# Attention in blocks of 32 queries by 64 keys, and three engines in written order, ahead of a PReLU feed-forward

## The chip, the cores and the metric

The kernel runs on one core of one Trainium2 chip. The metric is the time of one execution on the device in microseconds (us). Before the change it is 992.74 us, the median of 3 runs (988.51 to 993.65). Five engines work side by side: PE (TensorE, matrix products; PEld are its weight loads), DVE (VectorE), ACT (ScalarE), POOL (GpSimd) and SP, which issues the DMAs.

## The reference

Eight batches of 576 tokens, 8 heads of 64. Heads 0 to 3 look back at the last 32 positions, heads 4 to 7 at every fourth of the last 128. A feed-forward of 512 x 2048 x 512 with a PReLU follows.

```python
scores = scale * np.matmul(q, k.transpose(0, 1, 3, 2))
mask_plain = (rel >= 0) & (rel < window)                                   # window = 32
mask_dil = (rel >= 0) & (rel < window * dilation) & (rel % dilation == 0)  # dilation = 4
scores = np.where(masks[None, :, :, :], scores, -1000000000.0)
attn = np.exp(scores - np.max(scores, axis=-1, keepdims=True))
attn = attn / (np.sum(attn, axis=-1, keepdims=True) + 1e-09)
attn_out = np.matmul(attn, v)
...
h = x @ w_in                                          # x: 4608 x 512
g = np.maximum(h, 0.0) + alpha * np.minimum(h, 0.0)
return g @ w_out
```

## The kernel before

**Feed-forward.** The 4608 tokens are cut into 9 tiles of 512, the 2048 hidden values into 16 chunks, so there are 144 steps; step n is tile n // 16, chunk n % 16. `ffn_h` (L259) makes one 128 x 512 block of h with 12 matmuls (4 chunks of the model width, 3 passes each: every fp32 operand is kept as a high and a low fp32r part, and high x high, high x low and low x high are added). `ffn_g` (L264 to L277) applies the PReLU and casts the high part of g on ACT, `ffn_low` (L283) subtracts the low part on DVE, and `ffn_y` (L291) adds g's chunk to four output blocks with 12 matmuls. y runs one step behind h while tile 0 is done, two steps behind after that. After chunk 15 four blocks go out by DMA.

**Attention.** The work is cut by batch, pair of heads c (4 of them; the two heads lie on the lower and upper 64 partitions) and half u of the sequence: 64 units of 3 blocks, each block 96 queries by 128 keys. For the dilated heads tokens are sorted by residue modulo 4 beforehand, so that both kinds are a band. A unit goes through `scores` (L124, 6 fp32 matmuls; the profile shows each as two MATMUL records), `maxima` (L139, DVE adds the mask and takes the maximum), `exponentials` (L148, ACT), `divisions` (L155 to L158, DVE), `transposes` (L165, 6 on PE), `copies` (L170, ACT), `values` (L177, 6 fp32 matmuls), `highs` (L210, ACT) and `lows` (L214, DVE), which write the high and low parts of x.

**Weights.** They arrive as float64 in 32 chunks of 512 KB, and `convert_weight` (L238 to L247) makes each into a high and a low fp32r chunk: a magnitude on ACT (L238), four operations on the two words on DVE (L239, L240, L242, L244), the high cast on ACT (L246), the low part on DVE (L247).

**Order.** Batch 0 runs ahead of the first step, with 4 of the 32 conversions beside it. The 16 steps of tile 0 carry the other 28, two a step, and the 8 units of batch 1. From step 16 on a step is 24 matmuls of the feed-forward, and two steps share one unit of attention until batch 7 is through. The order on PE, DVE and ACT is set by a scheduler from the order of the code, so independent instructions are mixed; each engine then runs its queue in order. PSUM has 8 banks: four under the tag "y" (the output blocks; before step 1 the scores of batch 0) and four under "a" (h, scores, transposes and values, in rotation: a new tile takes the bank of the fourth tile before it). Weights in their float64 form and g share four buffers (tag "g"). DMAs wait in the queue of SP.

Of the kernel before, what the change touches and what calls it, by code (L numbers as in the profile page):

```python
# [9 lines left out]
F32 = mybir.dt.float32  # L10
# [12 lines left out]
BQ = 96  # L23
NBLK = S // BQ
UB = 3
UQ = UB * BQ
# [17 lines left out]
F64_HIGH = float.fromhex("0x1.dffffep16")  # L44


@with_exitstack
def tile_window_attention_prelu_ffn(
# [29 lines left out]
    ident = const.tile([BQ, BQ], F32, name="ident")  # L78
    make_identity(nc, ident)
    mask_sb = const.tile([BQ, NMASK, P], F32, name="mask_sb")  # L80
    al = const.tile([P, NF], F32, name="al")
    nal = const.tile([P, NF], F32, name="nal")
    wi = const.tile([P, 2, NF, NC, P], F32R, name="wi")
# [11 lines left out]
    keys = {}  # L95

    class Unit:
        def __init__(self, b, c, u, banks="a", room=None):
            self.b, self.c, self.u, self.banks = b, c, u, banks
            self.plain = 2 * c < HP  # L100
            self.blocks = range(UB * u, UB * (u + 1))
            self.starts = PLAIN_START if self.plain else DIL_START
            self.kinds = PLAIN_KIND if self.plain else DIL_KIND
            self.id = f"{b}_{c}_{u}"
            self.room = room

        def load(self):
            b, c, u = self.b, self.c, self.u
            if u == 0:
                keys[b, c] = att.tile([P, S], F32, tag="k", name=f"k_{b}_{c}")  # L110
                nc.sync.dma_start(out=keys[b, c], in_=kT[b, c])
            self.k = keys[b, c]
            self.q = att.tile([P, UQ], F32, tag="q", name=f"q_{self.id}", bufs=3)
            nc.sync.dma_start(out=self.q, in_=qT[b, c, :, u * UQ:(u + 1) * UQ])
            self.v = att.tile([P, 2, UB, D], F32, tag="v", name=f"v_{self.id}", bufs=3)
            nc.sync.dma_start(out=self.v, in_=vW[b, c, u])

        def scores(self):

            self.ps = [psp.tile([BQ, UB, P], F32, tag=self.banks, name=f"s_{self.id}_{e}") for e in range(2)]  # L120
            for i, j in enumerate(self.blocks):
                for e in range(2):
                    rows = slice(e * D, (e + 1) * D)
                    nc.tensor.matmul(  # L124
                        self.ps[e][:, i, :], lhsT=self.q[rows, i * BQ:(i + 1) * BQ],
                        rhs=self.k[rows, self.starts[j]:self.starts[j] + P], start=True, stop=True,
                    )

        def maxima(self):

            self.nm = sml.tile([BQ, 2, UB], F32, tag="nm", name=f"nm_{self.id}")
            if self.room is not None:
                self.pr = self.room
            else:
                pr = [att.tile([BQ, UB, P], F32, tag="pr", name=f"pr_{self.id}_{e}", bufs=3) for e in range(2)]
                self.pr = pr
            for e in range(2):
                for i, j in enumerate(self.blocks):
                    nc.vector.tensor_tensor_reduce(  # L139
                        out=self.pr[e][:, i, :], in0=self.ps[e][:, i, :], in1=mask_sb[:, self.kinds[j], :],  # L140
                        scale=-SCALE, scalar=3.0e38, op0=ALU.add, op1=ALU.min, accum_out=self.nm[:, e, i:i + 1],
                    )

        def exponentials(self):
            self.sm = sml.tile([BQ, 2, UB], F32, tag="sm", name=f"sm_{self.id}")
            for e in range(2):
                for i in range(UB):
                    nc.scalar.activation(  # L148
                        out=self.pr[e][:, i, :], in_=self.pr[e][:, i, :], func=AF.Exp,
                        bias=self.nm[:, e, i:i + 1], scale=-1.0, accum_out=self.sm[:, e, i:i + 1],  # L150
                    )

        def divisions(self):
            rs = sml.tile([BQ, 2, UB], F32, tag="rs", name=f"rs_{self.id}")
            nc.vector.tensor_scalar_add(rs, self.sm, 1e-9)  # L155
            nc.vector.reciprocal(out=rs, in_=rs)
            for e in range(2):
                nc.vector.tensor_tensor(  # L158
                    out=self.pr[e], in0=self.pr[e], in1=rs[:, e, :, None].broadcast_to([BQ, UB, P]), op=ALU.mult)

        def transposes(self):
            self.tp = [psp.tile([P, UB, BQ], F32, tag="a", name=f"t_{self.id}_{e}") for e in range(2)]
            for e in range(2):
                for i in range(UB):
                    nc.tensor.transpose(out=self.tp[e][:, i, :], in_=self.pr[e][:, i, :], identity=ident)  # L165
# [294 lines left out]
```

## Time and profile before

| | before |
|---|---|
| median of 3 runs | 992.74 us (988.51 to 993.65) |
| the profiled execution | 995.82 us |
| its span, first to last instruction | 993.9 us |
| DVE busy / ACT busy in the span | 580.9 us / 382.9 us |
| mean granted TensorE clock | 0.972 |
| moved by DMA | 58.78 MB |

The profile is of one execution, on the one core. Busy time is the time in which an instruction of the engine runs, "PEclk" the share of full clock that TensorE was granted. In the lists of groups a row has the line, the engine, the operation, output <- inputs, the shape, the count, busy time and the mean of one. A timeline row has start, duration and what ran, with the idle time before it and what ended that in brackets.

### The profile page before, as it was taken

The page shows a single profiled execution, that of the slowest core. Times are in us where ns is not written, and L with a number is a line of the kernel's source. Part 1 is how long each engine was busy: PE and PEld are TensorE (multiplying, and loading weights), DVE is VectorE, ACT ScalarE, POOL GpSimd, SP SyncE. Part 2 cuts the span into 40 slices and gives each one's busy share as a digit, 9 for nine tenths or more (in the row PEclk, how much of TensorE's full clock was granted, in tenths as well). Part 3 has the DMA queues.
Part 4 walks back from the last instruction along what each step waited for, and adds up shares of the span by engine and source line. Part 5 has one row for each costly group of instructions (what it writes and reads, how often), then busy time and mean ns, then how long its engine had stood idle before and what let it go on. Part 6 is the DMA issues. An engine that isn't in the chain of part 4 may idle for free.

```text
span 993.9 us, 14724 instructions
## 1 busy us (share of the span) xinstructions
PE 964.2 (97%) x5388; PEld 770.4 (78%) x5388; DVE 580.9 (58%) x1732; ACT 382.9 (39%) x1267; POOL 0.6 (0%) x6
## 2 busy tenths in 40 slices
PE   7699999999999999999999999999999999999998
PEld 4466766788888888888888888888888888888886
DVE  5869899755555556655555556555555544434343
ACT  5757667533433334433343334333433321111111
POOL 0000000000000000000000000000000000000000
PEclk8579899999999999999999999999999999999999
DMA  7334543211112111211121112111121001001001
GB/s 234 116 104 163 164 156 125 83 41 40 41 38 67 33 41 40 83 41 41 41 82 36 32 41 83 41 41 40 41 74 32 1 1 43 1 1 43 0 1 43
DMA packets 39303, 58.78 MB, mean 59 GB/s; under 512 B 3808, under 2 KB 28480, under 8 KB 39232
## 3 DMA queue, kind: packets, MB, share of 16 engines
q1 hardware_dynamic: 39232, 57.84, 18.6%
q8 instruction: 43, 0.70, 0.3%
q14 instruction: 28, 0.23, 0.1%
HBM read 48.39 MB, written 9.44 MB: 58 GB/s over the span
## 4 chain that ended last, share of the span: by engine, by line
PE 88%; DVE 7%; ACT 2%; issue 1%; DMA 1%; SPq 0%; ACTq 0%
PE h L259 38%; PE y L291 37%; PE s L124 5%; PE o L177 4%; PE t L165 3%; DVE wa L244 1%; DVE wa L242 1%; DVE wa L239 1%; DMA q<-qT 1%; DVE pr L139 1%; ACT early L148 1%; DVE wi L247 1%; DVE pr L158 1%; DVE wo L247 1%; DVE m L271 1%
## 5 line engine op out<-in xcount | busy, mean ns | idle before, releaser
L291 PE MATMUL y<-g,wo 128*128 128x512 f32 x1728 | 431.1, 397 | 7.2 <-ACT g L277 7.2
L259 PE MATMUL h<-x,wi 128*128 128x512 f32 x1728 | 427.4, 397 | 0.0
L259 PEld LDWEIGHTS h<-x,wi 128*128 128x128 f32 x1728 | 331.2, 192 | 69.8 <-issue 0.4
L291 PEld LDWEIGHTS y<-g,wo 128*128 128x128 f32 x1728 | 315.8, 188 | 81.4 <-ACT g L277 10.6
L274 DVE TENSOR_SCALAR m<-h,al 128x512 f32<-128x512 f32 x128 | 96.1, 751 | 278.8 <-PE h L259 274.2
L277 ACT CAST g<-m 128x512 fp32r<-128x512 f32 x144 | 89.5, 621 | 188.5 <-DVE m L275 185.8
L283 DVE TENSOR_TENSOR g<-m,g 128x512 fp32r<-128x512 f32 x144 | 99.1, 688 | 55.8 <-ACT g L277 55.6
L148 ACT ACTIVATE pr<-pr,nm 96x128 f32<-96x128 f32 x336 | 130.8, 392 | 2.3 <-DVE nm L139 2.2
L210 ACT CAST x<-o 128x288 fp32r<-128x288 f32 (+8 forms) x112 | 36.0, 393 | 218.3 <-PE o L177 218.3
L170 ACT COPY pt<-t 128x288 f32<-128x288 f32 x128 | 46.2, 400 | 141.7 <-PE t L165 141.2
L275 DVE SCALAR_TENSOR_TENSOR m<-h,m 128x512 f32<-128x512 f32 x128 | 88.5, 692 | 4.4
L139 DVE CUSTOM_DVE_ANT_0 pr<-s,mask_sb 96x128 f32<-96x128 f32 x336 | 75.2, 281 | 0.0
L124 PE MATMUL s<-k,q 64*96 64x128 f32 x768 | 62.2, 290 | 5.1 <-DMA q<-qT 5.1
L148 ACT ACTIVATION_READ_ACCUMULATOR pr<-pr,nm 96x1 f32 x336 | 63.6, 189 | 0.0
L158 DVE TENSOR_TENSOR pr<-pr,rs 96x384 f32<-96x384 f32 x112 | 57.7, 550 | 1.7
L124 PEld LDWEIGHTS s<-k,q 64*96 64x96 f32 x768 | 47.1, 165 | 14.8 <-issue 6.7
L177 PEld LDWEIGHTS o<-pt,v 128*64 128x64 f32 x768 | 37.2, 143 | 23.9 <-issue 20.5
L177 PE MATMUL o<-pt,v 128*64 128x96 f32 x768 | 50.9, 264 | 0.6 <-ACT pt L170 0.2
L165 PEld LDWEIGHTS t<-ident,pr 96*128 96x128 f32 x336 | 34.4, 142 | 15.2 <-DVE pr L158 8.1
L165 PE MATMUL t<-ident,pr 96*128 96x96 f32 x336 | 40.2, 252 | 4.2 <-DVE pr L158 4.1
L214 DVE TENSOR_TENSOR x<-o,x 128x288 fp32r<-128x288 f32 (+8 forms) x112 | 41.4, 383 | 3.7 <-ACT x L210 3.7
L139 DVE DVE_READ_ACCUMULATOR2_ANT nm<- 96x1 f32 x384 | 30.4, 79 | 0.0
(33 smaller groups left out, 281.6 us busy)
## 6 DMA issues: line engine op xcount, KB each, us to landing
v<-vW SPq DMA_DIRECT2D x64, 192.0 KB, 2.3
k<-kT SPq DMA_DIRECT2D x32, 288.0 KB, 3.2
q<-qT SPq DMA_DIRECT2D x64, 144.0 KB, 2.8
out<-ob SPq DMA_DIRECT2D x36, 256.0 KB, 2.2
ws<-w_in SPq DMA_DIRECT2D x16, 512.0 KB, 3.6
ws<-w_out SPq DMA_DIRECT2D x16, 512.0 KB, 3.5
mask_sb<-masks SPq DMA_DIRECT2D x1, 144.0 KB, 3.6
al<-alpha SPq DMA_DIRECT2D x1, 8.0 KB, 3.2
```

The costliest lines, as they stand in the source:

```text
L124: nc.tensor.matmul(self.ps[e][:, i, :], lhsT=self.q[rows, i * BQ:(i + 1) * BQ], rhs=self.k[rows, self.starts[j]:self.starts[j] + P], start ...
L139: nc.vector.tensor_tensor_reduce(out=self.pr[e][:, i, :], in0=self.ps[e][:, i, :], in1=mask_sb[:, self.kinds[j], :], scale=-SCALE, scalar= ...
L148: nc.scalar.activation(out=self.pr[e][:, i, :], in_=self.pr[e][:, i, :], func=AF.Exp, bias=self.nm[:, e, i:i + 1], scale=-1.0, accum_out=s ...
L158: nc.vector.tensor_tensor(out=self.pr[e], in0=self.pr[e], in1=rs[:, e, :, None].broadcast_to([BQ, UB, P]), op=ALU.mult)
L165: nc.tensor.transpose(out=self.tp[e][:, i, :], in_=self.pr[e][:, i, :], identity=ident)
L177: nc.tensor.matmul(self.po[e * D:(e + 1) * D, i, :], lhsT=self.v[:, e, i, :], rhs=self.pt[e][:, i, :], start=True, stop=True,)
L259: nc.tensor.matmul(ps, lhsT=wi[:, a, f, c, :], rhs=x[:, c, e, :], start=(n == 0), stop=(n == 3 * NC - 1))
L274: nc.vector.tensor_scalar(out=m, in0=ps, scalar1=0.0, scalar2=al[:, f:f + 1], op0=ALU.min, op1=ALU.mult)
L275: nc.vector.scalar_tensor_tensor(out=m, in0=ps, scalar=0.0, in1=m, op0=ALU.max, op1=ALU.add)
L277: nc.scalar.copy(out=g[:, 0, :], in_=m)
L283: nc.vector.tensor_tensor(out=g[:, 1, :], in0=ms.pop((t, f)), in1=g[:, 0, :].bitcast(F32), op=ALU.subtract)
L291: nc.tensor.matmul(ys[t][c], lhsT=wo[:, a, f, c * P:(c + 1) * P], rhs=g[:, e, :], start=(f == 0 and n == 0), stop=(f == NF - 1 and n == 2),)
```

## The change

1. Attention is cut into blocks of 32 queries by 64 keys, and a pair of heads of one batch (`Pair`, both halves at once) takes the place of a unit: 32 pairs. A score block uses 64 rows and 32 columns of the array, so the matmuls of a pair go to 8 parts of it in turn; a value block uses 64 rows and 64 columns, 4 parts. Four blocks of a column group fill 128 partitions, so a pair has 12 maxima (64 elements wide, 8 of them on 128 partitions and 4 on 32), 10 exponentials, 2 multiplications in the divisions, 5 transposes and 2 copies.
2. PE, DVE and ACT run in the order of the code (`manual_schedule`); SP's order is still set by the scheduler.
3. `convert_weight` is split into `magnitude`, `words`, `high` and `low`. Ten chunks are converted beside batch 0, the other 22 in steps 0 to 10, two a step.
4. The loop is laid out anew: a pair every fourth step (scores and the values of the pair before in the same step), h of the next step issued at the end of a step. The ReLUs of tile 0 write back into PSUM. Tag "m" has 5 buffers. alpha is loaded behind weights, q, k and v of the opening.
5. v comes with the 64 keys of each block: 576 KB a pair instead of 2 x 192 KB.

```diff
-BQ = 96
-UB = 3
+BQ = 32
+BK = 2 * BQ
+HB = 9
+NG = 4
+NR = 2 * NG + 2
...
+    ctx.enter_context(tc.manual_schedule(engines={nc.tensor.engine, nc.vector.engine, nc.scalar.engine}))
...
+        def score(self, e, g, col, j):
+            rows = slice(e * D, (e + 1) * D)
+            nc.tensor.matmul(
+                self.ps[e][col * BQ:(col + 1) * BQ, g, :], lhsT=self.q[rows, j * BQ:(j + 1) * BQ],
+                rhs=self.k[rows, first_key(j):first_key(j) + BK], start=True, stop=True,
+            )
...
+            for g in range(NG):
+                for m in range(4):
+                    for e in range(2):
+                        self.score(e, g, m, HB * (g % 2) + 4 * (g // 2) + m)
+                if g < 2:
+                    for e in range(2):
+                        self.score(e, NG + g, e, HB * g + HB - 1)
...
         def values(self):
+            self.po = [psp.tile([P, HB, BQ], F32, tag="a", name=f"o_{self.id}_{u}") for u in range(2)]
+            for j in range(HB):
+                for u in range(2):
+                    for e in range(2):
+                        rows = slice(u * BK, (u + 1) * BK)
...
+                            self.po[u][e * D:(e + 1) * D, j, :], lhsT=self.v[rows, e, j, :], rhs=pt[:, :BQ],
...
+    nc.sync.dma_start(out=al, in_=alpha)
+    w0 = conversion()
+    pairs[0].scores()
+    w0.words()
+    w0.high()
     nc.vector.tensor_scalar_mul(nal, al, -1.0)
+    load()
+    for s in range(NC):
+        u = pairs[s]
+        pairs[s + 1].scores()
+        if s:
+            pairs[s - 1].copies()
+            pairs[s - 1].values()
+        u.maxima()
+        u.exponentials(0, 4)
+        w1 = conversion()
+        u.exponentials(4)
+        w0.low()
+        w1.words()
+        load()
+        if s:
+            pairs[s - 1].highs()
+        w1.high()
+        if s:
+            pairs[s - 1].lows()
+        w2 = conversion()
+        u.divisions()
+        u.transposes()
+        w2.words()
+        load()
+        w1.low()
+        w2.high()
+        w0 = w2
...
+    at = {4 * (p - NC) - 2: p for p in range(NC, B * NC)}
...
+        if begin:
+            ffn_sum(t, f)
+            ffn_high(t, f)
+            if late:
+                late.low()
+            if n:
+                ffn_y(*pending.pop(0))
...
+            if scored:
+                scored.scores()
+            if valued:
+                valued.values()
+            if w1:
+                w1.words()
+                w1.high()
+                load()
+            w2 = conversion()
+            if scored:
+                scored.maxima()
...
+            ffn_h(*divmod(n + 1, NF))
+            if n + 1 < NF:
+                ffn_relu(t, f + 1)
...
+            ffn_low(t, f)
+            if w1:
+                w1.low()
+            if w2:
+                w2.words()
+                w2.high()
+                load()
+            late, w1 = w2, conversion()
+        else:
+            ffn_parts(t, f)
+            ffn_high(t, f)
+            if divided:
+                divided.divisions()
+            if turned:
+                turned.transposes()
+                turned.copies()
+            ffn_low(t, f)
+            while len(pending) >= 2:
+                ffn_y(*pending.pop(0))
+            if scored:
+                scored.scores()
+            if valued:
+                valued.values()
+            if scored:
+                scored.maxima()
+                scored.exponentials(0, 4)
...
+            if n + 1 < NTILE * NF:
+                ffn_h(*divmod(n + 1, NF))
```

PE before, in the stage of the feed-forward at full pace: the queue between the h of one step and the h of the next (o are the values of one unit, s the scores of the next; behind them y of two steps before, and after the next h the transposes t).

```order
L259 MATMUL h_7_5175<-x_3048,wi 128x512 x12
L177 MATMUL o_1_1_5188<-pt_1_1_0_5149,v_1_1_4937 64x96
L177 MATMUL o_1_1_5188<-pt_1_1_1_5150,v_1_1_4937 64x96
...
L124 MATMUL s_2_0_0_5195<-k_2_5051,q_2_0_5053 96x128
L124 MATMUL s_2_0_1_5196<-k_2_5051,q_2_0_5053 96x128
...
L291 MATMUL y_0_4919<-g_5_5088,wo 128x512 x3
...
L259 MATMUL h_8_5244<-x_3048,wi 128x512 x12
L165 MATMUL t_2_0_0_5257<-ident,pr_2_0_0_5209 128x96 x3
```

The same place of the changed kernel: y of two steps before comes first, then 36 scores that alternate between the heads, then 36 values, then at once the next h.

```order
L338 MATMUL y_3_3163<-g_8_3593,wo 128x512 x3
L129 MATMUL s_3_0_3681<-k_3_3550,q_3_3552 32x64
L129 MATMUL s_3_1_3682<-k_3_3550,q_3_3552 32x64
...
L204 MATMUL o_2_0_3719<-pt_2_0_3602,v_2_3548 64x32
L204 MATMUL o_2_0_3719<-pt_2_1_3603,v_2_3548 64x32
L204 MATMUL o_2_1_3720<-pt_2_0_3602,v_2_3548 64x32
...
L297 MATMUL h_11_3789<-x_1043,wi 128x512 x12
```

The 12 matmuls of y that stood between the scores and the next h have moved ahead of the scores.

SP at the start of the program before (k, q, v of the first two units, the mask, alpha as `al`, then weights as `ws`):

```order
L111 DMA k_0_101<-kT 128x576
L114 DMA q_0_0_103<-qT 128x288
L116 DMA v_0_0_105<-vW 128x384
L322 DMA mask_sb<-masks 96x384
L114 DMA q_0_1_108<-qT 128x288
L116 DMA v_0_1_110<-vW 128x384
L324 DMA al<-alpha 128x16
L223 DMA ws_0_114<-w_in 128x4x256
L223 DMA ws_1_116<-w_in 128x4x256
L111 DMA k_1_118<-kT 128x576
```

And of the changed kernel:

```order
L251 DMA ws_0_107<-w_in 128x4x256
L118 DMA k_0_109<-kT 128x576
L120 DMA q_0_111<-qT 128x576
L382 DMA mask_sb<-masks 128x256
L251 DMA ws_1_114<-w_in 128x4x256
L118 DMA k_1_116<-kT 128x576
L120 DMA q_1_118<-qT 128x576
L125 DMA v_0_120<-vW 128x1152
L253 DMA ws_0_122<-w_out 128x1024
L387 DMA al<-alpha 128x16
```

Three weight chunks, all of q and k of two pairs and the v of one now stand ahead of alpha. On DVE of the changed kernel the instruction that reads alpha (`nal`) comes behind the first conversion and ahead of the first maximum (the rows behind `nal` are maxima, pr, and their results, nm):

```order
L272 TENSOR_SCALAR wa_0_125<-wa_0_125 128x512
L273 TENSOR_SCALAR wa_0_125<-wa_0_125 128x512
L275 SCALAR_TENSOR_TENSOR wa_0_125<-ws_0_107,wa_0_125 128x512
L277 SCALAR_TENSOR_TENSOR wa_0_125<-ws_0_107,wa_0_125 128x512
L392 TENSOR_SCALAR nal<-al 128x16
L154 ISA pr_0_212,nm_0_211<-s_0_0_127,mask_sb 128x64
L154 ISA nm_0_211 128x1
```

Before, `nal` was the second instruction of DVE, behind a memset; four instructions of a conversion now stand ahead of it, each working on the result of the one before.

More of the change, by code (lines that the diff above doesn't have):

```diff
@@ L92, in cell, with __init__ @@
         return cells[t]
[L95 to L99, printed above, removed]
+    class Pair:
+        def __init__(self, b, c, banks="a", pr=None, v=None):
+            self.b, self.c, self.banks = b, c, banks
             self.plain = 2 * c < HP
[L101 to L116, printed above, removed]
-        def scores(self):
[L120 to L126, printed above, removed]
-                    )
[L129 to L151, printed above, removed]
@@ L155, in divisions @@
             nc.vector.tensor_scalar_add(rs, self.sm, 1e-9)
             nc.vector.reciprocal(out=rs, in_=rs)
-            for e in range(2):
[L158 to L165, printed above, removed]
+            for rows, a, z in ((slice(0, P), 0, 2 * NG), (slice(0, 2 * BQ), 2 * NG, NR)):
+                nc.vector.tensor_tensor(
+                    out=self.pr[rows, a:z], in0=self.pr[rows, a:z],
+                    in1=rs[rows, a:z, None].broadcast_to([rows.stop, z - a, BK]), op=ALU.mult)
@@ L311, in tile_window_attention_prelu_ffn, with load @@
             wq.append((0, f + 2))
-    early = xp.tile([P, NC * 2 * TT], F32, tag="x", name="early")
-    first = []
-    for n, (c, u) in enumerate((c, u) for c in range(NC) for u in range(2)):
-        k = n % 5
-        room = [
-            early[:BQ, (2 * k + e) * UB * P:(2 * k + e + 1) * UB * P].rearrange("p (i n) -> p i n", i=UB)
-            for e in range(2)]
-        first.append(Unit(0, c, u, banks="y", room=room))
+    loads, convs = list(wq), list(wq)
+    def load():
+        if loads:
+            load_weight(*loads.pop(0))
@@ new lines, in conversion @@
+    def conversion():
+        if not convs:
+            return None
+        w = Conversion(*convs.pop(0))
+        w.magnitude()
+        return w
+    early = xp.tile([P, NC * 2 * TT], F32, tag="x", name="early")
+    vsize = 2 * HB * D
+    pairs = [Pair(b, c, banks="y" if b * NC + c <= NC else "a") for b in range(B) for c in range(NC)]
+    for i in range(1, NC):
+        pairs[i].v = early[:, (i - 1) * vsize:i * vsize].rearrange("p (e j d) -> p e j d", e=2, j=HB)
+        if i % 2:
+            pairs[i].pr = early[:, 3 * vsize:3 * vsize + NR * BK].rearrange("p (r k) -> p r k", r=NR)
@@ L370, in tile_window_attention_prelu_ffn, with due @@
+    u, v = pairs[NC - 1], pairs[NC]
+    w1 = conversion()
+    u.copies()
+    u.values()
+    v.maxima()
+    u.highs()
+    w0.low()
+    v.exponentials()
+    u.lows()
+    w1.words()
+    w1.high()
+    load()
+    v.divisions()
+    at = {4 * (p - NC) - 2: p for p in range(NC, B * NC)}
+    def due(n):
+        return pairs[at[n]] if n in at else None
     pending = []
+    late, w1 = w1, conversion()
     for n in range(NTILE * NF):
@@ L373, in tile_window_attention_prelu_ffn @@
         begin = t == 0
-        lag = 1 if begin else 2
-        load, score, trans, value = todo[n]
-        for u in load:
-            u.load()
-        ffn_h(t, f)
-        for u in value:
-            u.values()
-        for u in score:
-            u.scores()
-        for u in trans:
-            u.transposes()
-            u.copies()
-        ffn_g(t, f, begin)
-        for u in score:
-            u.maxima()
-        for u in value:
-            u.highs()
-        for u in score:
-            u.exponentials()
@@ L393, in tile_window_attention_prelu_ffn @@
[L393 to L407 removed]
+        for u in [due(n + 3)] + ([due(n + 2)] if n == 0 else []):
+            if u:
+                u.load_qk()
```

321 lines of the change are left out of this document (179 added, 142 removed).

## The prediction

> **What bounds the kernel now.** I read the page first, then busy time by stage, then the timeline of one stretch.
>
> ```profile
> PE 964.2 (97%) x5388; PEld 770.4 (78%) x5388; DVE 580.9 (58%) x1732; ACT 382.9 (39%) x1267; POOL 0.6 (0%) x6
> ...
> PE 88%; DVE 7%; ACT 2%; issue 1%; DMA 1%; SPq 0%; ACTq 0%
> PE h L259 38%; PE y L291 37%; PE s L124 5%; PE o L177 4%; PE t L165 3%; DVE wa L244 1%; DVE wa L242 1%; DVE wa L239 1%; DMA q<-qT 1%; DVE pr L139 1%; ACT early L148 1%; DVE wi L247 1%; DVE pr L158 1%; DVE wo L247 1%; DVE m L271 1%
> ```
>
> PE ends the chain for 88% of the span; 75 of these points are the feed-forward, which the change leaves alone, 12 are attention on PE. The share is an average, so here are the stages (start:end, length, busy time of PE, PEld, DVE, ACT, POOL, granted clock, DMA).
>
> ```profile
> 8.00:49.00 41.00, 27.83 (x217) 20.51 (x213) 32.31 (x159) 31.25 (x131) 0.00 (x0) 0.66 0.54 172
> 49.00:182.40 133.40, 122.07 (x635) 91.48 (x635) 116.53 (x328) 87.84 (x239) 0.00 (x0) 0.90 0.42 135
> 182.40:808.00 625.60, 625.57 (x3711) 504.87 (x3710) 357.09 (x1140) 238.09 (x860) 0.00 (x0) 1.00 0.15 46
> ```
>
> Up to 182.4 us, where step 16 begins, no engine is full, and DVE (116.5 of 133.4) is the fullest for its work: its instructions depend on each other, and PE waits for it. From there to 808 PE has no gap, at full clock; what is taken off PE there is gained, and DVE (57%) and ACT (38%) have room. Behind 808 there is only feed-forward. One period of the middle stage and two steps without attention:
>
> ```profile
> 400.70 3.02 PE L291 MATMUL y<-g,wo 128*128 128x512 f32 x12
> 403.55 2.89 PE L259 MATMUL h<-x,wi 128*128 128x512 f32 x12
> 406.28 0.66 PE L165 MATMUL t<-ident,pr 96*128 96x96 f32 x6
> 406.72 3.01 PE L291 MATMUL y<-g,wo 128*128 128x512 f32 x12
> 409.57 2.88 PE L259 MATMUL h<-x,wi 128*128 128x512 f32 x12
> 412.38 0.72 PE L177 MATMUL o<-pt,v 128*64 128x96 f32 x12
> 413.02 0.90 PE L124 MATMUL s<-k,q 64*96 64x128 f32 x12
> ...
> 810.49 2.88 PE L259 MATMUL h<-x,wi 128*128 128x512 f32 x12
> 813.21 2.88 PE L291 MATMUL y<-g,wo 128*128 128x512 f32 x12
> 815.93 2.88 PE L259 MATMUL h<-x,wi 128*128 128x512 f32 x12
> ```
>
> Without attention a step takes 815.93 - 810.49 = 5.44 us, 2.72 a group. With it, from h at 403.55 to the y behind s (413.02 + 0.83 = 413.85; y runs 0.13 late behind fp32 work, as 403.55 - 400.70 = 2.85 shows) two steps take 13.15: a unit costs 13.15 - 10.88 = 2.27 us of PE, a pair of heads **4.54**. From step 16 on 23.5 pairs remain: 107 us, the pool from which the change can draw.
>
> **Part 1, the pair on PE.** What does a matmul on a part of the array cost? The same timeline asked in slices, with the count of o's MATMULs that run in each:
>
> ```profile
> 412.50:412.52 0.02, 0.02 (x4) 1.00 0.00 0
> 412.52:412.59 0.07, 0.07 (x4) 1.00 0.00 0
> 412.59:412.61 0.02, 0.02 (x6) 1.00 0.00 0
> ```
>
> Two start together (one for each head's half of the columns), then none for 70 ns, then two. So the parts work side by side, and each streams 96 columns in (0.72 - 0.25) / 6, about 0.08 us; s, with 128, in about 0.11. That is 0.85 ns a column: 55 ns for a score of 64 columns, 27 ns for a value of 32. If all 8 and 4 parts overlap, 72 score records make 9 rounds, 0.5 us, and 72 value records 18 rounds, 0.5 us. The other limit is how fast PE's queue hands them over. After a stall it starts empty:
>
> ```profile
> 13.33 0.39 PEld L124 LDWEIGHTS s<-k,q 64*96 64x96 f32 x3 [5.05 <-issue]
> ...
> L165 PEldq EVENT_SEMAPHORE  x1: 51/51/51, 13.4 to 13.4; - x1
> ```
>
> The second row (line 165 asked between 13.42 and 13.43 us) is the semaphore instruction of the transposes, queued behind the six score matmuls that begin at 13.33. Six fp32 matmuls, 12 records, have left the queue in 0.1 us: **8 ns a record** is the lower bound for the pace. The upper is 43 ns, the pace at which o runs now (0.47 us over 11 intervals). I take the lower, since it is read where the array does not set the pace; at 8 ns the array and the queue bind alike.
>
> Clock: the middle stage keeps its 1.00 if PE stays without gaps.
>
> A new wait comes in. The banks of tag "a" go round in four: the h behind the values takes the bank of the first head's scores, and must wait for that head's 6 maxima. Queued behind it on PE is everything, y of the next step first. In written order DVE has done its part of the step by then.
>
> ```profile
> 414.24 0.28 DVE L139 CUSTOM_DVE_ANT_0 pr<-s,mask_sb 96x128 f32<-96x128 f32 x1
> 414.45 0.08 DVE L139 DVE_READ_ACCUMULATOR2_ANT nm<- 96x1 f32 x1
> 414.45 0.28 DVE L139 CUSTOM_DVE_ANT_0 pr<-s,mask_sb 96x128 f32<-96x128 f32 x1
> ...
> L283 DVE TENSOR_TENSOR g<-m,g 128x512 fp32r<-128x512 f32 x144 | 99.1, 688 | 55.8 <-ACT g L277 55.6
> ...
> L158 DVE TENSOR_TENSOR pr<-pr,rs 96x384 f32<-96x384 f32 x112 | 57.7, 550 | 1.7
> ```
>
> A maximum comes every 0.21 us for 128 elements, and 128 elements more cost (688 - 550) ns, so 64 fewer save 0.07: 0.14 each, bounded by 0.21 (nothing saved). From the first score: 0.5 of streaming, 0.1 of start, 0.27 to the end of the last, 6 x 0.14 = 0.84, and about 0.25 for the hand-overs: h may start at **1.97 us**. The values end their streaming near 1.3 and lie beneath that wait, even at three times their time. With 0.1 to change shape before s and 0.13 behind, 2.2. The transposes: 6 of 96 columns took 0.44, so 5, four of them 128 wide, about 0.5, and 0.15 for changes of shape: 0.65. Sum **2.85 us a pair** against 4.54: (4.54 - 2.85) x 23.5 = **39.7 us**. Bounds: 2.3 if the wait is gone, 3.3 if a maximum still costs 0.21. DVE and ACT, with fewer and wider instructions, are covered by PE in this stage; their gain is nothing.
>
> **Part 2, the opening.** alpha comes later, and `nal` holds DVE ahead of the first maximum.
>
> ```profile
> 3.54 0.43 SPq L324 DMA_DIRECT2D al<-alpha  x1
> ...
> 6.76 0.18 DVE L325 TENSOR_SCALAR nal<-al 128x16 f32<-128x16 f32 x1 [5.36 <-DMA al<-alpha]
> ...
> 5.59 7.64 DMA q<-qT
> ...
> 5.00:10.00 5.00, 3.50 (x29) 1.90 (x27) 2.30 (x22) 1.79 (x9) 0.00 (x0) 1.00 0.92 278
> 10.00:15.00 5.00, 1.64 (x13) 1.39 (x14) 1.91 (x11) 2.93 (x16) 0.00 (x0) 0.57 0.88 318
> ```
>
> DMAs land in the order of their issue: q, issued at 5.59 behind two weight chunks, took 7.64 us. Behind 3392 KB (3 x 512 + 4 x 288 + 128 + 576) at about 300 GB/s alpha lands near 14 us, 7 later than now. From there DVE decides. Conversions are now chains:
>
> ```profile
> 47.61 0.42 DVE L240 TENSOR_SCALAR wa<-wa 128x512 uint32<-128x512 uint32 x1
> 48.06 0.69 DVE L242 SCALAR_TENSOR_TENSOR wa<-ws,wa 128x512 uint32<-128x512 uint32 x1
> 48.79 0.69 DVE L244 SCALAR_TENSOR_TENSOR wa<-ws,wa 128x512 uint32<-128x512 uint32 x1
> ...
> 100.12 0.68 DVE L247 TENSOR_TENSOR wi<-wa,wi 128x512 fp32r<-128x512 f32 x1
> 100.72 0.68 DVE L242 SCALAR_TENSOR_TENSOR wa<-ws,wa 128x512 uint32<-128x512 uint32 x1
> ```
>
> Dependent ones follow at 0.45 and 0.73, independent ones at 0.60: a conversion takes 0.45 + 0.45 + 0.73 + 0.60 for its words and 0.60 for its low part, 2.83 (mixed by the scheduler, 2 x 0.34 + 3 x 0.60 = 2.48). The rest of a pair:
>
> ```profile
> L148 ACT ACTIVATE pr<-pr,nm 96x128 f32<-96x128 f32 x336 | 130.8, 392 | 2.3 <-DVE nm L139 2.2
> ...
> L214 DVE TENSOR_TENSOR x<-o,x 128x288 fp32r<-128x288 f32 (+8 forms) x112 | 41.4, 383 | 3.7 <-ACT x L210 3.7
> ```
>
> Lows: 41.4 us of busy time over 32 pairs is 1.3, about 1.2 in time since neighbours overlap. Divisions: 550 ns for 384 elements makes about 0.7 for 512, with the narrow ones 1.2. On ACT ten exponentials of at most 0.39 and two casts and two magnitudes of about 0.6 each come to some 7.5 us a round with copies and highs, less than DVE has; ACT is late only where DVE asks for the next magnitude behind four exponentials. A round of batch 0 on DVE is thus 12 maxima (1.7), two conversions (5.7), divisions (1.2), lows (1.2) and some 0.5 of waits: 10.3; the first, without lows and waits, 8.6. The last pair takes maxima, lows, one conversion's words and low part, divisions and 1.5 for PE and ACT: 8.4. So the first PReLU sum comes at 14 + 8.6 + 30.9 + 8.4 = 62 us. A round loads 2176 KB (two chunks, one pair), 216 GB/s over 10.3 us, below the 278 to 318 of the rows: DMA is covered.
>
> In the steps of tile 0 DVE needs 0.67 + 0.60 for the feed-forward and 5.66 for two conversions, 6.93, and now in 11 steps, not 14: 76 us, plus three pairs (11) and some 4 where the low part waits for ACT: 153. The five steps left run at PE's pace: behind the h then running (to 156) 7 groups of 2.72 and one and a half pairs, so step 16 starts between 177 and 180.
>
> ```profile
> 182.41 2.88 PE L259 MATMUL h<-x,wi 128*128 128x512 f32 x12
> ```
>
> Before it was 182.41. I book **-3 us**. Bounds: -15 if alpha does not wait its turn and conversions cost no more than mixed ones (7 and 0.35 x 32 = 11, less what then falls to PE), +9 if each of the 15 rounds and steps waits another 0.8. The larger v (576 KB for 384 a pair) and the single buffers of v, pr and pt are covered in the middle stage: DMA is at 15% there, and each buffer is read two steps or more before it is written again.
>
> **Sum.** 995.8 (the profiled execution: 993.9 and 1.9 around it) - 39.7 - 3 = 953; the median of the runs lies 3.1 below that execution: **950 us**.
>
> **Rivals.** *Two parts at a time.* The rows show two parts side by side, never four or eight. Then scores take 36 x 0.055 = 2.0, values 36 x 0.027 = 1.0, shapes 0.5, transposes 0.65: 4.1 a pair, 10 us gained, 980. For it: weight loads of more parts may share a path. Against: nothing in the rows shows an order between the two parts.
>
> *The pace of records, halfway.* At 25 ns a record, between 8 and 43, 144 records take 3.6, with 1.17 for shapes and transposes 4.77 a pair: +5 - 3, so **995**, no change. The Trainium skill, "TensorE: Matmul & The Clock Gate", section "Wait — 56ns, not 53.3ns?", says that starts of matmuls never come closer than about 25 ns, however few columns; by that rule this is the time. The trace speaks against it: the two starts within one 20 ns slice above.
>
> *The pace of o now* ends slower. If each record keeps 43 ns whatever its width, a pair takes 144 x 0.043 + 1.17 = 7.4, so +66 and about 1056; it decides from (4.67 - 1.17) / 144 = 24 ns a record. For it: 288 records of matmul and load in one burst, where the longest now is 48. Against: the 0.1 us above.
>
> **How the numbers follow.** 66% for the forecast (926 to 972 by its bounds: 2.3 to 3.3 a pair, -15 to +9 in the opening), 12% for two parts, 7% for halfway, 15% for a pace above it. The range takes in the first two: 926 to 990. A difference under 0.5% (988 to 998 is "same") cannot be told from none. Faster 0.77 (the forecast and nearly all of two parts), same 0.09, slower 0.14.
>
> **What would show it.** Right: from step 16 on PE without gaps, save about 0.5 us ahead of the h behind the values, released by DVE's maxima; s and o near 0.8 us each; four steps in 21.76 + 2.85 = 24.6 us; `nal` near 14 us; step 16 near 178. Wrong: s and o stretched to 2 us or more, starts at an even 25 or 43 ns, a granted clock below 1.00 in the middle stage, or step 16 past 190.

## The result, and the profile after

| | before | after |
|---|---|---|
| median of the runs | 993.19 us (988.51 to 994.46, 4 runs) | 964.50 us (964.16 to 965.19, 4 runs) |
| profiled execution, its span | 995.82, 993.9 | 965.19, 963.4 |
| h of step 16 starts | 182.41 | 184.71 |
| from there to the h of the last step | 796.73 | 763.91 |

After stands to before as 0.972 (95% interval 0.9688 to 0.9753): 28.7 us less, where 43 were forecast. Behind step 16 the span lost 796.73 - 763.91 = 32.8 us; ahead of it 184.71 - 182.41 = 2.3 came back.

The page of after, busy times and shares of the chain of waits:

```profile
PE 908.4 (94%) x8236; PEld 740.1 (77%) x8236; DVE 528.5 (55%) x1606; ACT 306.4 (32%) x1075; POOL 0.7 (0%) x6
...
PE 85%; DVE 10%; ACT 3%; DMA 1%; issue 0%
```

PE has 56 us less to do, yet the end came only 30 earlier: DVE's share of the chain rose from 7 to 10%. Busy time by stage (PE, PEld, DVE, ACT, POOL, clock, DMA) shows where:

```profile
8.00:49.00 41.00, 17.21 (x519) 14.62 (x519) 32.80 (x151) 24.97 (x109) 0.00 (x0) 0.52 0.76 275
49.00:184.70 135.70, 110.43 (x1045) 86.66 (x1046) 111.03 (x315) 77.70 (x227) 0.00 (x0) 0.92 0.36 117
184.70:808.00 623.30, 623.30 (x5921) 511.13 (x5920) 321.71 (x1050) 182.67 (x708) 0.00 (x0) 1.00 0.17 55
```

Behind step 16 PE is full at clock 1.00, as before, so all that it was relieved of counts. Ahead of it PE lost 11.6 us of work (122.07 to 110.43 from 49 us on) and stood still for 25.3 us instead of 11.3. The timeline of after on PE, two stretches of one period:

```profile
406.58 2.89 PE L297 MATMUL h<-x,wi 128*128 128x512 f32 x12
409.31 0.60 PE L183 MATMUL t<-ident,pr 128*128 128x128 f32 x4
409.84 0.27 PE L186 MATMUL t<-ident,pr 64*128 64x64 f32 x1
410.04 3.02 PE L338 MATMUL y<-g,wo 128*128 128x512 f32 x12
412.90 0.39 PE L297 MATMUL h<-x,wi 128*128 128x512 f32 x1
...
421.06 2.88 PE L338 MATMUL y<-g,wo 128*128 128x512 f32 x12
423.87 0.98 PE L129 MATMUL s<-k,q 64*32 64x64 f32 x72
424.78 1.25 PE L204 MATMUL o<-pt,v 64*64 64x32 f32 x72
425.98 2.99 PE L297 MATMUL h<-x,wi 128*128 128x512 f32 x12
428.81 2.88 PE L338 MATMUL y<-g,wo 128*128 128x512 f32 x12
```

Take 2.72 off each feed-forward group. The transposes then cost 412.90 - 406.58 - 2 x 2.72 = 0.88 us, scores and values 428.81 - 421.06 - 2 x 2.72 = 2.31: a pair 3.2 us, where 2.85 were forecast (0.65 and 2.2). A period of four steps, h to h, has 24.95 to 24.97 us, so 3.2 a pair; forecast were 24.6 and 2.85.

### The profile page after: what moved, and what is told of

It reads as the page before. It is cut to its first block, busy times and chain, and to the rows that moved or that the text cites. A ratio compares the mean times of both kernels' runs of the same rounds, so it can differ in the third digit from the quotient of the medians.

```text
span 963.4 us, 19961 instructions
## 1 busy us (share of the span) xinstructions
PE 908.4 (94%) x8236; PEld 740.1 (77%) x8236; DVE 528.5 (55%) x1606; ACT 306.4 (32%) x1075; POOL 0.7 (0%) x6
## 4 chain that ended last, share of the span: by engine, by line
PE 85%; DVE 10%; ACT 3%; DMA 1%; issue 0%
PE h L297 39%; PE y L338 38%; PE o L204 3%; PE s L129 2%; DVE wa L275 2%; DVE wa L277 2%; DVE wa L273 1%; PE t L183 1%; DVE wa L272 1%; DVE wi L284 1%; ACT wi L281 1%; DVE wo L284 1%; DMA ws<-w_out 1%; DVE pr L154 1%; ACT pr L162 1%; ACT wo L281 1%
## 5 line engine op out<-in xcount | busy, mean ns | idle before, releaser
L338 PEld LDWEIGHTS y<-g,wo 128*128 128x128 f32 x1728 | 322.0, 188 | 82.2 <-DVE g L330 14.7
L162 ACT ACTIVATE pr<-pr,nm 128x64 f32<-128x64 f32 x300 | 100.3, 340 | 47.1 <-DVE nm L154 47.1
L154 DVE CUSTOM_DVE_ANT_0 pr<-s,mask_sb 128x64 f32<-128x64 f32 x360 | 56.3, 213 | 19.0 <-PE s L129 18.0
L162 ACT ACTIVATION_READ_ACCUMULATOR pr<-pr,nm 128x1 f32 x300 | 57.5, 192 | 0.0
L129 PEld LDWEIGHTS s<-k,q 64*32 64x32 f32 x2304 | 28.1, 110 | 15.0 <-ACT g L325 6.0
L204 PE MATMUL o<-pt,v 64*64 64x32 f32 x2088 | 37.8, 223 | 0.7 <-ACT pt L194 0.6
L129 PE MATMUL s<-k,q 64*32 64x64 f32 x2304 | 33.5, 235 | 4.5 <-DMA q<-qT 4.5
L204 PEld LDWEIGHTS o<-pt,v 64*64 64x64 f32 x2088 | 34.5, 137 | 3.9 <-ACT pt L194 0.8
L154 DVE DVE_READ_ACCUMULATOR2_ANT nm<- 128x1 f32 (+1 forms) x384 | 28.9, 75 | 0.0
L172 DVE TENSOR_TENSOR pr<-pr,rs 128x512 f32<-128x512 f32 (+1 forms) x60 | 26.6, 485 | 1.0
L275 DVE SCALAR_TENSOR_TENSOR wa<-ws,wa 128x512 uint32<-128x512 uint32 x32 | 22.2, 692 | 1.1
```

The source lines that it names most:

```text
L129: nc.tensor.matmul(self.ps[e][col * BQ:(col + 1) * BQ, g, :], lhsT=self.q[rows, j * BQ:(j + 1) * BQ], rhs=self.k[rows, first_key(j):first_ ...
L154: nc.vector.tensor_tensor_reduce(out=self.pr[rows, r, :], in0=self.ps[e][rows, g, :], in1=mask_sb[rows, kind, :], scale=-SCALE, scalar=3.0 ...
L162: nc.scalar.activation(out=self.pr[rows, r, :], in_=self.pr[rows, r, :], func=AF.Exp, bias=self.nm[rows, r:r + 1], scale=-1.0, accum_out=s ...
L204: nc.tensor.matmul(self.po[u][e * D:(e + 1) * D, j, :], lhsT=self.v[rows, e, j, :], rhs=pt[:, :BQ], start=True, stop=True,)
L275: nc.vector.scalar_tensor_tensor(out=a, in0=hi, scalar=0xC0000000, in1=a, op0=ALU.bitwise_and, op1=ALU.bitwise_or)
L338: nc.tensor.matmul(ys[t][c], lhsT=wo[:, a, f, c * P:(c + 1) * P], rhs=g[:, e, :], start=(f == 0 and n == 0), stop=(f == NF - 1 and n == 2),)
```

## The experiments

Each is made from the kernel after and measured beside before; ratios are to before. After itself stands at 0.972. The start of step 16 is a coarse measure of the opening: in e1 and e4, which leave DVE's order there as it is, it comes at 183.94 and 186.06 us, 184.71 in after.

### What sets the pace of a part of the array

Values were forecast at 27 ns a matmul pass in each part, 0.5 us a pair. They take 1.25 us with 0.22 for the last one alone, 1.03 for 72 starts. The trace has these starts one by one, in ns, at the beginning of the values:

```
424779 424786 424792 424799   424858 424865 424871 424878   424916 424923 424930 424936   424975 ...
```

Four starts come 6 to 7 ns apart, read here as one for each part (e4 below, with two parts in turn, has two), then none for 38 ns (59 the first time): a round lasts 58.3 ns, twice the forecast. Two edits ask what fills it.

**e1_wide_moving** streams 64 columns past the same weights, in place of 32.

```diff
...
+    w = 2 if j < HB - 2 else 1
-    self.po[u][e * D:(e + 1) * D, j, :], lhsT=self.v[rows, e, j, :], rhs=pt[:, :BQ],
+    self.po[u][e * D:(e + 1) * D, j:j + w, :], lhsT=self.v[rows, e, j, :], rhs=pt[:, :w * BQ],
```

> Seven of nine value matmuls of each part stream 64 columns in place of 32 (the second block is written over by the next matmul, so the output is the same). Now four parts start every 58.3 ns, 1.03 us for a pair. (a) The weight load sets the part's period and lies beside the stream: 64 columns stream in 55 ns, below 58, so the rounds stay at 58 ns, o at 1.03 us, and the time at 964 to 966. (b) Load or a fixed 31 ns comes behind the stream: rounds of 55 + 31 = 86 ns, 14 of 18, o at 1.4 us, +0.38 us a pair on PE, 973 us. (c) The queue hands over a record every 14.6 ns: no change, as (a).

963.47 us, ratio 0.971 (0.9685 to 0.9735). Its timeline on PE:

```profile
198.50 0.98 PE L129 MATMUL s<-k,q 64*32 64x64 f32 x72
199.41 1.25 PE L205 MATMUL o<-pt,v 64*64 64x64 f32 x72
200.62 2.76 PE L298 MATMUL h<-x,wi 128*128 128x512 f32 x11
```

Twice the columns cost nothing: o 1.25 as before, h 2.12 behind the first score. (b) is out; the stream is not what fills the round.

**e2_narrow_weights** loads 32 columns of weights for each value matmul. It computes only half of each head's outputs; two wide matmuls a part fill the other half with other values.

```diff
...
-    self.po[u][e * D:(e + 1) * D, j, :], lhsT=self.v[rows, e, j, :], rhs=pt[:, :BQ],
+    self.po[u][e * D:e * D + BQ, j, :], lhsT=self.v[rows, e, j, :BQ], rhs=pt[:, :BQ],
```

> The 72 value records load 32 columns of weights in place of 64, and so compute only the first 32 of each head's 64 outputs; the other 32 columns of each part are filled ahead of them by two wide matmuls, whose values are not the reference's. (a) The load sets the period: it halves, rounds of about 30 to 40 ns, 72 records in 0.55 to 0.7 us. (b) Load behind stream: 27 + 15 = 42 ns, 0.76 us. (c) Queue: 58 ns still, 1.03 us, and with 16 more records some 1.2. In all three h starts no earlier than 2.0 us behind the first score, since DVE's sixth maximum ends there: the time gains at most 0.1 us a pair, 962 to 965; where the wait does not bind, (a) would gain up to 0.4 us a pair, 955.

Its timeline on PE, in a pair without disturbance (L204 is the filling, L213 the narrow matmuls):

```profile
255.97 0.98 PE L129 MATMUL s<-k,q 64*32 64x64 f32 x72
...
257.37 0.70 PE L213 MATMUL o<-pt,v 64*32 64x32 f32 x55
258.08 3.00 PE L306 MATMUL h<-x,wi 128*128 128x512 f32 x12
```

The last 55 of the 72 records start within 0.70 - 0.19 = 0.51 us, 9.4 ns each; where they run evenly two start every 16.7 ns. A round of four takes 33 to 38 ns instead of 58. Fewer columns of weights, shorter rounds: (a) holds, the weight load fills the round, and (c), a queue at 14.6 ns, is out. The Trainium skill, "TensorE: Matmul & The Clock Gate", section "LDWEIGHTS (loading the stationary operand)", gives a load's time in ns as its columns over 1.2, which makes, as an estimate, 53 for 64 columns and 27 for 32. The rows give 58 and 33 to 38, near it in the first case; the second may be held by something else too, such as a pace of 8 ns a record, which the prediction had read for PE's queue.

The time went the other way, 971.25 us (ratio 0.9777, 0.975 to 0.9803): in 4 of 23 pairs behind step 16 PE stood still for 1.6 to 1.8 us near the end of the values. The trace puts three of these stalls down to "issue" and one to maxima that had long been done. Each ends 2.5 to 2.7 us behind the start of a transfer of 16 KB on DMA queue 8, which the profile lists as instructions (transfers at 202.00, 228.72, 581.51 and 608.10 us, ends at 204.60, 231.26, 584.15 and 610.79), and so does a fifth stall in the opening (176.30, 178.94). So PE probably waited for its own next instructions; no run tests that. Behind the second stall the granted clock fell as well, to 0.64 between 231.5 and 236.2 us, and h took 4.61 us instead of 2.88.

In the other 19 pairs h starts 2.11 us behind the first score, as in after, although the values end 0.04 us earlier: there the maxima hold it. So this run settles the pace, and its time says nothing on the load.

**e4_two_parts** runs the same matmuls with two parts taking turns, so that the rival "two parts at a time" comes about by the order alone.

```diff
-    for g in range(NG):
-        for m in range(4):
+    for m in range(4):
+        for g in range(NG):
             for e in range(2):
                 self.score(e, g, m, HB * (g % 2) + 4 * (g // 2) + m)
-        if g < 2:
-            for e in range(2):
-                self.score(e, NG + g, e, HB * g + HB - 1)
+    for g in range(2):
+        for e in range(2):
+            self.score(e, NG + g, e, HB * g + HB - 1)
...
-    for j in range(HB):
-        for u in range(2):
+    for u in range(2):
+        for j in range(HB):
```

> The same matmuls in an order in which only two parts take turns (scores: one group of columns after the other; values: one half of the rows after the other). If parts run beside each other and each has a period of its own (55 ns for a score, 58 for a value), 72 score records take 36 x 55 = 2.0 us and 72 value records 36 x 58 = 2.1 us: about +2.3 us a pair on PE, 54 us, 1015 to 1020 us, slower than before the change. If the queue's pace sets s and o (10.6 and 14.6 ns a record), nothing changes: 964 to 968.

995.86 us, ratio 1.0047 (1.0022 to 1.0071): the order alone takes the whole gain away.

```profile
200.62 1.45 PE L129 MATMUL s<-k,q 64*32 64x64 f32 x72
202.00 2.09 PE L204 MATMUL o<-pt,v 64*64 64x32 f32 x72
204.02 2.34 PE L297 MATMUL h<-x,wi 128*128 128x512 f32 x9
```

From the first score to h 3.40 us, 1.29 more than in after; times 23.5 that is 30, and the time rose by 31. From first to last start the values took 1.87 us, where 2.1 were expected, since the second half of the rows begins before the first is through. Scores took 1.24 in place of 2.0: the starts show a new group of columns beginning while the group before still has about half of its matmuls to go, so that four parts run for most of the time. Read by parts, each starts a score every 56 ns, as forecast.

**e7_full_transposes** gives the fifth transpose all 128 rows (the unused 64 are set to zero once).

```diff
...
-    out=self.tp[0][:, 2 * P:], in_=self.pr[:2 * BQ, 2 * NG:, :].rearrange("q h k -> q (h k)"),
-    identity=ident[:2 * BQ, :2 * BQ])
+    out=self.tp[0][:, 2 * P:], in_=self.pr[:, 2 * NG:, :].rearrange("q h k -> q (h k)"),
+    identity=ident)
```

> The fifth transpose of a pair takes all 128 rows (the 64 unused ones are set to zero once) and gives 128 columns, of which the first 64 are used. If its 0.20 us ahead and 0.20 behind are the price of changing from the full array to a part of 64 rows and back, they go: 0.11 for its 128 columns and about 0.03 behind it, as the transposes of before had, so 0.25 to 0.3 us a pair, 6 to 7 us in all, 957 to 959. If the gaps belong to going from transposes to matmuls whatever the shape, it costs 0.05 more a pair: 965 to 966.

957.32 us, ratio 0.965 (0.9612 to 0.9688).

```profile
403.51 2.89 PE L299 MATMUL h<-x,wi 128*128 128x512 f32 x12
406.23 0.60 PE L185 MATMUL t<-ident,room 128*128 128x128 f32 x4
406.67 0.27 PE L188 MATMUL t<-ident,room 128*128 128x128 f32 x1
406.69 3.01 PE L340 MATMUL y<-g,wo 128*128 128x512 f32 x12
409.54 2.88 PE L299 MATMUL h<-x,wi 128*128 128x512 f32 x12
```

y now starts 0.02 us behind the fifth transpose, not 0.20, and the transposes cost 409.54 - 403.51 - 5.44 = 0.59 us instead of 0.88. Behind step 16 this saves 763.91 - 757.35 = 6.6 us. The two gaps were the price of one small matmul of another shape. The Trainium skill, "TensorEngine Tiling (Array Packing)", section "Key Properties", says that a change of the tiling mode drains the engine; it gives no figure; here the two changes took 0.20 us each, and without them a pair is 0.29 us shorter.

### What sets the opening

**e3_alpha_first** loads alpha ahead of the second weight chunk.

```diff
     nc.sync.dma_start(out=mask_sb, in_=masks)
+    nc.sync.dma_start(out=al, in_=alpha)
...
-    nc.sync.dma_start(out=al, in_=alpha)
```

> alpha is loaded behind the masks, ahead of the second weight chunk. nal is then done near 7.9 us, behind w0's words, and the first maximum starts at about 8 instead of 14.82. If DVE sets the opening from there on without other waits, step 16 starts 6.8 us earlier, at 178, and the time is about 958. If the loads of batch 0 are late instead (pairs 1 and 2, the chunks), DVE waits for them and part comes back: a gain of 2 to 4 us, 961 to 963, with DMA as releaser of DVE, ACT or PE before 30 us.

959.91 us, ratio 0.9673 (0.9651 to 0.9694). DVE's row of `nal`, of after and then of e3, and h of step 16 in e3:

```profile
14.69 0.17 DVE L392 TENSOR_SCALAR nal<-al 128x16 f32<-128x16 f32 x1 [6.92 <-DMA al<-alpha]
```

```profile
7.88 0.17 DVE L392 TENSOR_SCALAR nal<-al 128x16 f32<-128x16 f32 x1
...
179.28 2.89 PE L297 MATMUL h<-x,wi 128*128 128x512 f32 x12
```

DVE starts 6.8 us earlier, the first PReLU sum 5.1 (59.24, 64.38 in after), step 16 5.4. The rest may have gone to a new wait: up to 70 us PE waits 9.5 us for q, not 4.5. A load of 8 KB in the wrong place was worth some 5 us (4.6 by the medians).

**e5_maxima_first** puts the maxima ahead of the words in tile 0's steps.

```diff
+    if scored:
+        scored.maxima()
     if w1:
         w1.words()
...
-    if scored:
-        scored.maxima()
```

> In the steps of tile 0 DVE takes the maxima ahead of the words of the step's first conversion. In steps 2, 6 and 10 the h behind the scores waits 2.3 to 2.7 us for the maxima (h at 83.50, 117.89, 152.28) and then runs slow. If this wait reaches the end only through DVE's next step, which waits about 0.5 us for the PReLU of that h, it is worth 3 x 0.5 = 1.6 us, 963. If PE sets the time from step 10 on, the last of the three waits counts in full: 2.2 + 2 x 0.5 = 3.2 us, 961. If DVE is the bound and its order makes no difference: 964.5, no change.

965.72 us, ratio 0.9736 (0.9698 to 0.9773): no gain. The h behind the scores of step 2 starts at 80.73 instead of 83.50, but steps 2 and 3 take 19.9 us together in both kernels: DVE has the same work, and its order moves PE's wait from one step to the next.

**e6_six_chunks** drops the second conversion from each round of batch 0; tile 0's steps convert two chunks until step 12, not 10.

```diff
-    w2 = conversion()
     u.divisions()
     u.transposes()
-    w2.words()
-    load()
-    w1.low()
-    w2.high()
-    w0 = w2
+    w0 = w1
```

> Six weight chunks instead of ten are converted beside batch 0, so the steps of tile 0 carry conversions up to step 12 instead of 10. If DVE's sum of work sets the opening, the conversions end no later than now while fewer steps of PE's work are left behind them: the first sum 4 x 2.85 = 11.4 us earlier, steps 11 and 12 longer by 9.42 - 5.44 and 7.26 - 6.61 us: step 16 near 178, 958 us. If the rounds of batch 0 are held by the chain maxima, exponentials, divisions, transposes, copies, values, highs, lows, and conversions only fill its waits, the rounds stay near 8 us, the first sum comes 4 to 6 us earlier, and step 16 near 184: 964, no change.

960.96 us, ratio 0.9687 (0.965 to 0.9725).

```profile
179.80 2.88 PE L297 MATMUL h<-x,wi 128*128 128x512 f32 x12
```

Step 16 starts 4.9 us earlier than in after, so the first theory's end came. Its way there was half right: the first PReLU sum came 6.8 us earlier (57.63, 64.38 in after), not 11.4, so the rounds seem to be partly held by their own chain. Ten chunks beside batch 0 cost 3.5 (by the medians) to 4.9 us (by step 16) against six: PE is busy for only 17 of 41 us there, and more is left for it behind.

**e8_mixed_words** and **e10_combined_mixed** take the chained words of a conversion apart by hand, the second behind the sum and together with e3, e6 and e7 (to be compared with e9, below).

```diff
+            if w1:
+                w1.words(0)
             ffn_sum(t, f)
             ffn_high(t, f)
+            if w1:
+                w1.words(1)
             if late:
                 late.low()
+            if w1:
+                w1.words(2)
+            ffn_low(t, f)
...
-                w1.words()
+                w1.words(3)
...
-            ffn_low(t, f)
+            if w2:
+                w2.words(0)
             if w1:
                 w1.low()
             if w2:
-                w2.words()
+                w2.words(1, 2, 3)
```

> In the steps of tile 0 the chained word operations of the conversions are taken apart, with the PReLU sum, the low parts of the chunk before and of g between them; the work is the same. A dependent neighbour costs 0.45 or 0.72 us from start to start, an independent one 0.34 or 0.60, so four gaps of 0.11 to 0.12 a step go, in 11 steps 5 us: 959 to 960, a step without attention 6.8 instead of 7.26 us. If DVE instead waits for ACT (the cast of g, now asked for earlier; the magnitudes), the step stays at 7.26: no change, 964 to 965.

> e9 and, in the steps of tile 0, the words of the first conversion taken apart by other work, but behind the PReLU sum, so that its magnitude on ACT has the time of the sum. Three dependent gaps of 0.11 to 0.12 us a step go. If the wait for the magnitude was all that cost e8_mixed_words its 16.6 us, a step without attention takes 6.9 instead of 7.26 us, and 13 steps give 4 us: 943 where e9 has 947. If DVE waits as well for the cast of g or for the magnitudes later in the step, nothing is gained or the step gets longer: 947 to 960.

981.10 us (ratio 0.9887, 0.9841 to 0.9933), 16.6 slower than after, and 962.67 (0.9705, 0.968 to 0.9731), 12.5 slower than e9. DVE's waits in the opening of e8, and in that of e10 (us, times, longest; `wa` is the chunk in conversion, the lines are its first word operation on DVE and its magnitude on ACT):

```profile
DVE wa L274 <- ACT wa L267: 26.2, 16, 4.4
```

```profile
DVE wa L276 <- ACT wa L269: 17.2, 17, 1.7
```

A conversion's first word waits for its magnitude on ACT, which stands behind the cast of the conversion before. In the order of the change the low parts and the sum lie just there and cover that way. After has no such wait from 60 us on. Half a microsecond a step was to be had, one to one and a half were paid.

**e12_scheduler** leaves the written order out, and nothing else: the new attention and the ten chunks in an order that the scheduler picks, as before the change.

```diff
-    ctx.enter_context(tc.manual_schedule(engines={nc.tensor.engine, nc.vector.engine, nc.scalar.engine}))
```

> The new attention and the ten chunks, but the order on PE, DVE and ACT is chosen by the scheduler again, as before the change. On DVE the middle stage stands in nearly the same order (12 maxima, low parts, PReLU, divisions), so a pair should cost the same there, 3.2 us. If the written order only decides the opening: the scheduler takes the conversions' chains apart (2.48 us in place of 2.85 for each of 32), up to 11 us in the opening, 953 to 960. If it asks DVE for words whose magnitudes ACT has not done, as e8_mixed_words did, or if it delays PE's feed-forward, 970 to 985. If the written order is worth nothing: 964 to 966.

947.02 us, ratio 0.9567 (0.9518 to 0.9617). Step 16, and the groups of two of the word operations over the whole run (busy, mean ns, idle ahead), of e12 and then of after:

```profile
167.55 2.89 PE L296 MATMUL h<-x,wi 128*128 128x512 f32 x12
...
L276 DVE SCALAR_TENSOR_TENSOR wa<-ws,wa 128x512 uint32<-128x512 uint32 x32 | 21.9, 685 | 0.0
L274 DVE SCALAR_TENSOR_TENSOR wa<-ws,wa 128x512 uint32<-128x512 uint32 x32 | 21.8, 680 | 0.0
```

```profile
L275 DVE SCALAR_TENSOR_TENSOR wa<-ws,wa 128x512 uint32<-128x512 uint32 x32 | 22.2, 692 | 1.1
L277 DVE SCALAR_TENSOR_TENSOR wa<-ws,wa 128x512 uint32<-128x512 uint32 x32 | 22.1, 692 | 1.1
```

Step 16 starts 17.2 us earlier than in after; from there to the last h it takes 763.93 us, after 763.91. The written order is worth nothing in the middle stage and costs 17 us in the opening. Of these, 7.4 are gone by the first sum (56.96 against 64.38): `nal` runs at 14.7 in both, but the scheduler lets the 12 maxima start at 7.86, ahead of it (e3 won 5.1 there by alpha alone). Another 8.6 go in the 11 steps with conversions (85.1 us against 93.7), where two conversions lie in each other's gaps:

```profile
68.60 0.42 DVE L272 TENSOR_SCALAR wa<-wa 128x512 uint32<-128x512 uint32 x1
68.94 0.42 DVE L271 TENSOR_SCALAR wa<-wa 128x512 f32<-128x512 f32 x1
69.27 0.69 DVE L274 SCALAR_TENSOR_TENSOR wa<-ws,wa 128x512 uint32<-128x512 uint32 x1
69.87 0.42 DVE L272 TENSOR_SCALAR wa<-wa 128x512 uint32<-128x512 uint32 x1
70.21 0.69 DVE L276 SCALAR_TENSOR_TENSOR wa<-ws,wa 128x512 uint32<-128x512 uint32 x1
```

Starts 0.34 and 0.60 apart, against 0.45 and 0.73 in a chain, and no wait: in contrast to e8 both magnitudes were there. Over the 11 steps DVE is busy for 78.3 us, against 87.0 in after, and idle for 6.8 against 6.7, so the gain is not fewer waits. Four word operations, some 2 us, have moved out of these steps; the other 6.7 us come from operations that follow each other sooner.

### Together

**e9_combined** is e3, e6 and e7 in the written order; **e13_best** is e6 and e7 in the scheduler's order.

> alpha behind the masks, six chunks beside batch 0 and full transposes together. By themselves they moved the last h by 5.4, 4.9 and 7.2 us. If they are independent (DVE's start, the split of DVE's work, PE in the middle stage), the sum is 17.5: 947 us. If alpha's earlier start and the lighter rounds of batch 0 spend the same time (rounds then held by the chain over ACT and PE, or by loads), only the larger of the two is left: 952.

> The scheduler's order with full transposes and six chunks beside batch 0. Full transposes are worth 6.6 us behind step 16 whatever stands ahead of it: 940. Six chunks leave PE less of its work behind the conversions only if DVE still sets the opening in the scheduler's order: then up to 5 us more, 935. If PE sets the opening from 50 us on already (119 of 128 us busy), six chunks bring nothing, 940; if the rounds of batch 0 are held by their own chain, the conversions moved out of them lengthen tile 0, and it is 942 to 946.

e9: 950.14 us, ratio 0.9577 (0.955 to 0.9605), between the two expectations. The gains nearly add up: by the medians e3, e6 and e7 won 4.6, 3.5 and 7.2 us, together 15.3, and e9 won 14.4; the first sum came 11.8 us earlier (52.62), where 5.1 and 6.8 were to be added. Step 16 moved by 8.2 us where 5.4 + 4.9 were to be added, but that difference is no larger than the scatter of step 16. So alpha and the rounds of batch 0 do not spend the same time, as far as these runs tell. e13: **934.39 us, ratio 0.94 (0.938 to 0.942)**, the fastest of all and 30 us below after. Step 16 starts at 161.50, 6 us ahead of e12: the six chunks pay in this order too.

## Why the prediction was right, and where its sizes were off

The forecast case came true: faster, by the mechanism named, inside the range, 14.5 us above the value given. By its steps:

- **PE stays full behind step 16, at clock 1.00**: held (623.30 of 623.30 us). The 0.5 us without work that was forecast ahead of h is missing: the values fill it.
- **Parts run side by side**: held. The rivals are out: two at a time is what e4 runs, and it costs 31 us; "halfway" and "the pace of o now" wanted 25 and 43 ns a record. The trace has 72 scores in 0.98 - 0.22 = 0.76 us, 10.6 ns each, and 14.5 for the values. The Trainium skill's rule of 25 ns between starts ("TensorE: Matmul & The Clock Gate", section "Wait — 56ns, not 53.3ns?") does not hold across parts: starts lie 6 to 7 ns apart.
- **"72 score records make 9 rounds, 0.5 us"**: the pace held (56 ns in e4), the count did not. The loop gives two of the 8 parts 6 of the 36 matmuls and the others 4, so the fullest part has 12 records, 0.67 us; the scores took 0.77, and where the last 0.1 comes from stays open. A shorter start and hand-over than booked made up for half of it: h was forecast 1.97 us behind the first score and comes at 2.11.
- **"27 ns for a value of 32"**: wrong, 58, set by the weight load. It was booked as hidden beneath the wait for the maxima even at three times its time, which its own terms do not give: from about 0.8 us on, three times 0.5 end at 2.3, behind the 1.97 of the wait. The sixth maximum's accumulator read ends at 425.76 + 0.07 = 425.83, 1.96 us behind the first score. The last value starts at 425.81. Both limits end together, and h follows, so the error cost little. That the values came out just as long as the wait is luck. Taking the wait away alone would gain almost nothing: in e4, where the sixth maximum is done 0.7 us ahead of the last value, h starts 0.15 us behind that value, here 0.17. DVE's rows there:

```profile
424.89 0.23 DVE L154 CUSTOM_DVE_ANT_0 pr<-s,mask_sb 128x64 f32<-128x64 f32 x1 [0.70 <-PE s L129]
425.04 0.08 DVE L154 DVE_READ_ACCUMULATOR2_ANT nm<- 128x1 f32 x1
...
425.62 0.21 DVE L154 CUSTOM_DVE_ANT_0 pr<-s,mask_sb 32x64 f32<-32x64 f32 x1
425.76 0.07 DVE L154 DVE_READ_ACCUMULATOR2_ANT nm<- 32x1 f32 x1
```

- **A maximum in 0.14 us**: held, 0.145.
- **"0.15 for changes of shape" in the transposes**: the term that was off in the middle stage. It was read from six transposes of one shape, and the fifth of the new ones has another. 0.88 instead of 0.65; e7 shows that the two changes are worth 0.29. With 0.11 for scores and values a pair takes 3.2: 0.35 x 23.5 = 8.2 us of the miss.
- **The opening, -3 us**: measured +2.3. `nal` came at 14.69 (forecast 14), the first sum at 64.38 (62): the last pair ahead of step 0 took 10.1 us from its maxima to the sum instead of 8.4, with 1.56 us of DVE waiting for ACT's highs behind values that took 2.41 us at a granted clock of 0.50. The steps with two conversions took 7.26 us (6.93), since the sum and g's low part come to 0.75 each. That makes 5.3 us late at step 16: 950 + 8.2 + 5.3 = 963.5, against 964.5 measured.
- **The lower bound of the opening, -15**, was worked out for an alpha that doesn't wait its turn and conversions in each other's gaps. e12 has both and stands at 167.55 - 182.41 = -14.9. The two prices were read nearly right (7 and 11 us, measured 7.4 and, in the 11 steps alone, 8.6, of which 6.7 by the order within them). They were booked as given, and so the order's own cost stood in the sum unseen.

So the change is two: the new attention, with its chunks and its loop, worth some 43 to 46 us in the scheduler's order (e12 against before beside it, 989.60 to 947.02, or against the 993 above), and the written order, which gives 17 of them back.

## What to carry to other kernels

Small matmuls on parts of the array run side by side, and then the weight load of each part, not its stream, can set the pace: count weight columns, order the matmuls so that all parts take turns, and never let a single one of another shape stand in a series. An order written out by hand freezes every wait in it, an 8 KB load and the latency of a dependent operation too: before keeping it, run the same program with the scheduler's order, and look at the stage that isn't bound by the engine that the order was written for.

## What the runs showed of the hardware that was not expected

- A part's period is 58.3 ns with 64 columns of weights, whether 32 or 64 columns stream past (after, e1), and 33 to 38 with 32 (e2).
- A transpose of 64 rows among those of 128 costs 0.2 us ahead of it and 0.2 behind; with 128 rows the next matmul follows in 0.02 us (after, e7).
- In e4 matmuls of the next group of columns start before the group in front is done, though each part keeps its own 56 ns.
- Stalls of PE of 1.6 to 1.8 us in 4 of 23 pairs of e2, each ending 2.5 to 2.7 us behind the start of a 16 KB instruction transfer; that it was the cause is not tested.
- In the 11 steps with conversions DVE is busy for 87.0 us with the words in chains and 78.3 us with them mixed and four of them fewer (after, e12): some 6.7 us come from nothing but which operation stands behind which.
